# Parameter and skip-term work of a two-branch state-space convolution moved off VectorE, with a redrawn order of work

## The chip, the cores and the metric

The kernel runs on one core of one Trainium2 chip. The metric is the device time of one execution in microseconds; lower is better. PE is the matrix engine (PEld its weight loads), DVE the vector engine, ACT the scalar engine, POOL GpSimd, and SP the engine that issues the DMAs here.

## The reference

Two state-space convolutions, A (S4) and B (S4D), read the same input `x` of length L = 2048 and D = 512 channels, each with N = 128 states per channel, and a gate mixes them:

```python
dt = jnp.exp(log_dt)[:, None]
A = A_re + 1j * A_im
P = jnp.exp((dt * A)[:, :, None] * l[None, None, :])
K = jnp.einsum("dn,dnl,dn->dl", Cc, P, dt * Bc).real      # branch A
...
K = 2.0 * jnp.einsum("dn,dnl->dl", C, P).real              # branch B
...
y = irfft(rfft(K, 2 * L) * rfft(u_t, 2 * L))[..., :L] + u * Dskip
...
g = sigmoid((x * gate_w).sum(-1, keepdims=True))
return g * a + (1 - g) * b
```

The skip term `u * Dskip` is a convolution with a kernel that has `Dskip` at lag 0, so it can be added to `K` at that one lag.

## The kernel before, in words

All arithmetic is fp32. The work is cut into four quarters of 128 channels and two branches: eight units `(q, k)`. A unit has eight chunks of 16 channels.

**Parameters of a quarter** (`params_t`, L366, and `params_c`, L405). States lie on the 128 partitions, channels on the columns, 256 columns for both branches. The raw rows arrive by DMA in a buffer of the pool AB. `params_t` spreads dt over the partitions: DVE makes two diagonal tiles (L370), a matmul with ones puts the spread steps into a PSUM bank (L375), ACT copies them to SBUF as `dtb` (L378), and the bank is free again. DVE then forms the decay rates `al` (L396) and the phases `pi` (L384 to L391) from `dtb`. `params_c` forms C times B (L415 to L418, DVE), magnitude and angle of the product (L425 and L426 on ACT, L431 to L436 on DVE, L444 to L446 on ACT), the amplitudes `pf` (L452 to L456, DVE), and the starting phases `fi` (L460 to L468, DVE; L476 to L480, POOL). Intermediates lie in SBUF tiles called p.

**Anchors** (L488). DVE scales `al` (L501, L502), and ACT takes 28 columns of exponentials per channel (L514) into an AB buffer; POOL multiplies the amplitudes in (L530).

**Chunk** (L535). POOL makes the phases x (L558 to L580) and the magnitudes E (L591, L599), ACT the four tables of sines, each in a PSUM bank (L609 to L617; one in the SBUF tile scs where the table DP gives its product to POOL), DVE or POOL the products Qt, Dt, Pt, Ct (L621 to L639), PE the kernel block `K` in PSUM (L654). ACT copies it to SBUF (L665), one or two chunks at a time, and DVE adds the skip values at column 31 of every channel's 64, lag 0 (L669).

**Transform.** Stage 1 (L692) transforms `K`, or the input, into F; the eviction of each bank is on DVE (L703) or ACT (L705), as the bit tables EV and EU say. `stage2` (L755) runs the forward step (L714), the complex product with the transformed input (L775, L778, DVE), the inverse step (L786, L787) and ACT's copy back into F (L792). `final` transposes on DVE (L808), runs the last matmuls (L814), applies the gate (L828, L830, L891, L856) and writes out.

**What sets the order.** A planner (`Plan.run`, L143) lists every operation with an engine, a cost and a due time, simulates the five queues with the buffers of each pool, and always starts the operation with the earliest due time among those whose inputs and buffers are ready. The order that comes out is the program order of each engine; on the chip each engine runs its queue in that order. So costs, latencies, due times and the numbers of buffers decide the order, though none of them is an instruction. PSUM is one pool of eight banks. A change of ACT's function table costs an extra instruction (ACT_TABLE_LOAD); SWITCH is the penalty that the planner puts on it.

Of the kernel before, what the change touches and what calls it, by code (L numbers as in the profile page):

```python
# [54 lines left out]
MT = 0.3  # L55
MA = 0.0
MV = 0.0
MG = 1.0
MD = 0.0
LAT = {"T": 0.2 + MT, "A": 0.14 + MA, "V": 0.13 + MV, "G": 0.08 + MG, "D": 0.95 + MD}  # L60
# [1 line left out]
LAG = (1.2, 0.75, 0.25, 0.4, 0.35, 0.35, 0.65, 0.55)
FSP = (0.6, 0.8, 1.1, 1.0, 1.3, 1.6, 0.9, 0.1)
YSP = (0.8, 0.8, 0.8, 0.8, 0.4, 0.8, 0.5, 0.2)
UDS = (-0.4, 0.2, 4.2, 0.7)
USP = (0.3, 0.8, 1.1, 0.9)
GD = 2.8
GSP = 0.3
DP = (1, 87, 20, 255, 128, 127, 13, 149)
# [1 line left out]
TWD = 1.4
UAHEAD = 0.5
UPRE = 0.7
WPRE = 0.8
AC = 5.0
AC2 = 4.0
PT = 3.0
PC = 3.0
# [1 line left out]
CV = 0.03  # L80
CD = 0.0
CK = 0.08
CE = 0.1
CS = 0.28
FW = 0.0
# [30 lines left out]
class Plan:  # L116
# [30 lines left out]
    def run(self):  # L147
# [15 lines left out]
        while n < len(self.ops):  # L163
            nxt = 1e30
            for e in at:
# [35 lines left out]
                if e == "T":  # L201
                    k = int((now - 0.14) / 3.413)
                    if k > win:
                        cold = (cold and busy < 0.8 * 3.413) or busy < 0.45 * 3.413
                        if k > win + 1:
                            left = max(0.0, at["T"] - 3.413 * (win + 1) - 0.14)
                            cold = cold or left < 0.45 * 3.413
                        win, busy = k, max(0.0, min(at["T"], now) - 3.413 * k - 0.14)
                    if cold:
                        cost *= 2  # L210
                    dens = 0.75 if o.cost in (1.27, 1.53) else 0.95
                    busy += dens * min(cost, 3.413 * (k + 1) + 0.14 - now)
# [35 lines left out]
def gated_s4_mix(ctx: ExitStack, tc: tile.TileContext, ins: dict, out: bass.AP):  # L248
# [111 lines left out]
    def params_t(q, due):  # L360
# [22 lines left out]
        theta = (
            (0.34, lambda: V.scalar_tensor_tensor(_flat(th()), _flat(th()), 1.0 / (2 * PI), dtb.t, ALU.mult, ALU.mult)),  # L384
            (0.2, lambda: V.tensor_scalar(t(), th(), MAGIC, MAGIC, ALU.add, ALU.subtract)),
            (0.34, lambda: V.tensor_tensor(th(), th(), t(), ALU.subtract)),
            (0.2, lambda: V.tensor_scalar(piv()[:, :, :, 0], th(), TWO32 / 2, None, ALU.mult)),
            (0.2, lambda: V.tensor_scalar(t(), th(), 64.0, MAGIC, ALU.mult, ALU.add)),
            (0.2, lambda: V.tensor_scalar(t(), t(), MAGIC, None, ALU.subtract)),
            (0.34, lambda: V.scalar_tensor_tensor(_flat(t()), _flat(th()), 64.0, _flat(t()), ALU.mult, ALU.subtract)),  # L390
            (0.2, lambda: V.tensor_scalar(piv()[:, :, :, 1], t(), TWO32, None, ALU.mult)),  # L391
# [11 lines left out]
    def params_c(q, due):  # L403

        w, d = raw[q], prm[q]  # L405
        t0, t1, t2, t3, fi = Buf("p"), Buf("p"), Buf("p"), Buf("p"), Buf("fi")
# [4 lines left out]

        def prod():
            W = rawv(w)
            CC = W[:, 4:8:2, :]
# [1 line left out]
            e.tensor_tensor(p3(t1), CC, W[:, 9:11, :], ALU.mult)
# [13 lines left out]
        ratio = (  # L430
            (0.34, lambda: V.tensor_tensor(p3(t0), aa(), p3(t2), ALU.max)),  # L431
            (0.34, lambda: V.tensor_tensor(p3(t1), aa(), p3(t2), ALU.min)),
            (0.34, lambda: V.tensor_tensor(p3(t2), p3(t2), aa(), ALU.is_gt)),
            (0.2, lambda: V.tensor_scalar(aa(), p3(t0), 1e-37, None, ALU.max)),
            (1.67, lambda: V.reciprocal(aa(), aa())),
            (0.34, lambda: V.tensor_tensor(aa(), p3(t1), aa(), ALU.mult)),  # L436
        )
# [21 lines left out]
        octants = (
            (0.2, lambda: V.tensor_scalar(x0(), aa(), -1.0 / PI, 0.25, ALU.mult, ALU.add)),  # L460
            (0.34, lambda: V.tensor_tensor(x0(), x0(), x2(), ALU.mult)),
            (0.34, lambda: V.scalar_tensor_tensor(_flat(aa()), _flat(aa()), 0.5 / PI, _flat(x0()), ALU.mult, ALU.add)),
            (0.2, lambda: V.tensor_scalar(x0(), aa(), -2.0, 0.5, ALU.mult, ALU.add)),
            (0.34, lambda: V.scalar_tensor_tensor(_flat(x0()), _flat(cr()), 0.0, _flat(x0()), ALU.is_lt, ALU.mult)),
            (0.34, lambda: V.tensor_tensor(aa(), aa(), x0(), ALU.add)),
            (0.2, lambda: V.tensor_scalar(x0(), ci(), 0.0, -2.0, ALU.is_lt, ALU.mult)),
# [7 lines left out]
        def middle():  # L474
# [5 lines left out]
            G.tensor_tensor(f, f, x, ALU.add)  # L480
# [604 lines left out]
```

## Time and profile before

| | |
|---|---|
| median of three runs | 547.89 us (542.36 to 551.44) |
| the profiled execution | 545.54 us, its span 543.8 us |
| mean granted PE clock | 0.948 |
| DVE busy | 500.6 us, 92% |
| PE / PEld busy | 443.3 / 384.4 us |
| POOL busy | 417.6 us, 77% |
| ACT busy | 411.8 us, 76% |
| DMA | 74.71 MB, 137 GB/s in the mean |

A row of instructions reads: line, engine, operation, output<-inputs by tile name, shapes, count | busy us, mean ns of one | idle time of the engine just before them, and what ended it. A row of one line by itself reads: minimum/median/maximum ns, first and last start. A row of stretches reads: from:to, its length, then the busy time of each engine with its number of instructions, the granted clock, the DMA share and GB/s; asked for one engine and one tile it has only that engine's busy time in instructions that touch the tile. A row of waits reads: who <- for whom: us in total, times, longest. ps is a PSUM bank. Busy times of successive DVE instructions overlap a little (0.68 us busy for a step of 0.60).

### The profile page before, as it was taken

How to read it: one execution, taken by the hardware profiler on the slowest of the kernel's cores; microseconds unless marked ns; L12 is line 12 of the kernel's file. 1: busy time of each engine (PE TensorE's matmuls, PEld its weight loads, DVE VectorE, ACT ScalarE, POOL GpSimd, SP SyncE). 2: the span in 40 equal slices, each digit the busy share in tenths (PEclk: the TensorE clock that was granted, in tenths of full speed). 3: DMA queues.
4: the chain of work that ended last, by engine and by line, in shares of the span. 5: the costliest groups of instructions: out<-in, count | busy, mean ns of one | idle time of the engine just before them, and what ended most of it. 6: DMA issues, size and time to landing. Idle time of an engine off the chain costs nothing. (4 is left out here: it accounts for less than half of the span.)

```text
span 543.8 us, 18151 instructions
## 1 busy us (share of the span) xinstructions
PE 443.3 (82%) x7640; PEld 384.4 (71%) x7640; DVE 500.6 (92%) x789; ACT 411.8 (76%) x779; POOL 417.6 (77%) x348
## 2 busy tenths in 40 slices
PE   2687977859887876868886995949899889999994
PEld 1686877759786655657676884949689668987981
DVE  6988989998989879999999999999899988999855
ACT  5799948859999765869786996847978989775224
POOL 2499979858997995677998499585999999994002
PEclk9979978989999997989998998878999999999999
DMA  8827343634334561522342474212345253422642
GB/s 284 320 70 228 116 150 94 196 101 139 118 98 137 186 220 40 161 94 86 134 153 66 151 264 140 71 30 83 133 139 154 96 175 106 155 80 86 220 143 80
DMA packets 35747, 74.71 MB, mean 137 GB/s; under 512 B 3792, under 2 KB 4176, under 8 KB 35408
## 3 DMA queue, kind: packets, MB, share of 16 engines
q1 hardware_dynamic: 35664, 73.54, 41.0%
q8 instruction: 60, 0.98, 0.8%
q14 instruction: 23, 0.19, 0.1%
HBM read 53.60 MB, written 19.92 MB: 135 GB/s over the span
## 5 line engine op out<-in xcount | busy, mean ns | idle before, releaser
L599 POOL TENSOR_TENSOR E<-AB 128x1024 f32<-128x1024 f32 x64 | 125.9, 1967 | 0.2
L786 PE MATMUL ps<-z,c_t 128*128 128x128 f32 x512 | 104.6, 287 | 14.1 <-DVE z L775 7.4
L714 PE MATMUL ps<-F,c_g 128*128 128x128 f32 x768 | 105.0, 287 | 9.6 <-DVE Qt L624 3.4
L714 PEld LDWEIGHTS ps<-F,c_g 128*128 128x128 f32 x768 | 95.6, 198 | 19.6 <-DVE Qt L624 3.6
L787 PE MATMUL ps<-z,c_t 128*128 128x128 f32 x512 | 101.6, 281 | 1.5 <-DVE z L778 1.4
L692 PE MATMUL ps<-w,K 128*64 128x128 f32 x1024 | 73.0, 298 | 31.2 <-DVE K L669 22.1
L786 PEld LDWEIGHTS ps<-z,c_t 128*128 128x128 f32 x512 | 79.1, 195 | 25.4 <-DVE z L775 8.6
L692 PEld LDWEIGHTS ps<-w,K 128*64 128x64 f32 x1024 | 62.4, 150 | 38.3 <-DVE K L669 24.8
L580 POOL TENSOR_TENSOR x<-pi,c_tm 128x512 int32<-128x512 int32 x64 | 69.1, 1080 | 20.0 <-ACT ps L613 14.4
L787 PEld LDWEIGHTS ps<-z,c_t 128*128 128x128 f32 x512 | 79.5, 196 | 2.5 <-DVE z L778 2.5
L634 DVE TENSOR_TENSOR Pt<-ps,E 128x1024 f32<-128x1024 f32 x64 | 77.6, 1212 | 2.7 <-PE ps L654 1.9
L654 PE MATMUL ps<-Pt,Ct 128*32 128x64 f32 x2048 | 66.0, 227 | 11.0 <-DVE Ct L639 8.3
L591 POOL TENSOR_TENSOR E<-AB 128x512 f32<-128x512 f32 x64 | 69.5, 1087 | 2.8 <-ACT AB L514 2.3
L571 POOL TENSOR_TENSOR x<-gh 128x512 int32<-128x512 int32 x64 | 69.4, 1085 | 0.1
L611 ACT ACTIVATE x<-x 128x1024 f32<-128x1024 int32 x64 | 68.0, 1063 | 1.6
L630 POOL TENSOR_TENSOR Dt<-scs,E 128x512 f32<-128x512 f32 x31 | 40.2, 1297 | 35.0 <-issue 26.6
L654 PEld LDWEIGHTS ps<-Pt,Ct 128*32 128x32 f32 x2048 | 47.9, 113 | 24.8 <-DVE Ct L639 12.5
L654 PE MATMUL ps<-Qt,Dt 128*32 128x64 f32 x2048 | 64.6, 224 | 0.0
L792 ACT COPY F<-ps 128x512 f32<-128x512 f32 x64 | 37.5, 587 | 31.3 <-PE ps L787 27.1
L514 ACT ACTIVATE AB<-al 128x128 f32<-128x128 f32 (+1 forms) x160 | 55.0, 535 | 5.2 <-DVE fi L468 3.0
L609 ACT ACTIVATE ps<-x 128x512 f32<-128x512 int32 x64 | 38.7, 604 | 22.1 <-DVE z L778 9.3
L775 DVE TENSOR_TENSOR z<-ps,U 128x512 f32<-128x512 f32 x64 | 43.4, 678 | 11.2 <-DMA U<-ud 9.1
(113 smaller groups left out, 898.9 us busy)
## 6 DMA issues: line engine op xcount, KB each, us to landing
U<-ud SPq DMA_DIRECT2D x64, 512.0 KB, 3.7
ud<-z SPq DMA_DIRECT2D x32, 256.0 KB, 2.7
U<-in_u SPq DMA_DIRECT2D x16, 256.0 KB, 4.0
ud<-z SPq DMA_DIRECT2D x32, 128.0 KB, 3.1
U<-in_uT SPq DMA_DIRECT2D x8, 512.0 KB, 4.0
c_t<-in_c_t SPq DMA_DIRECT2D x1, 3072.0 KB, 10.5
w<-st SPq DMA_DIRECT2D x12, 256.0 KB, 4.1
st<-w SPq DMA_DIRECT2D x12, 256.0 KB, 3.0
```

What stands on the lines that cost most here:

```text
L514: A.activation(dst()[..., i], src(), AF.Exp, scale=sg * float(t0 + dt * i))
L571: G.tensor_tensor(xi()[:, :, 1, :].rearrange("n c (a b) -> n c a b", a=4), t[:, :, 0:4].unsqueeze(3).to_broadcast([P, NCK, 4, 8]), t[:, :, ...
L580: lambda: G.tensor_tensor(xi()[:, :, 0, :], d["piv"]()[:, k, ch, 0].unsqueeze(2).to_broadcast([P, NCK, NJ]), tm[:, 0:NJ].unsqueeze(1).to_b ...
L591: G.tensor_tensor(Ev()[:, :, 0, :].rearrange("n c (a b) -> n c a b", a=4), A1()[:, ch, ::-1].unsqueeze(3).to_broadcast([P, NCK, 4, 8]), BB ...
L599: G.tensor_tensor(Ev()[:, :, 1:3, :].rearrange("n c w t -> n c (w t)"), AA()[:, ch].rearrange("n c w a -> n (c w) a").unsqueeze(3).to_broa ...
L611: op("A", 0.95, e, lambda: A.activation(x.t, x.v(dt=I32), AF.Abs), w=[x])
L634: lambda: V.tensor_tensor(qv(Pt), tv(cf).unsqueeze(2).to_broadcast([P, NCK, 2, NJ]), Ev()[:, :, 0:2, :], ALU.mult),
L654: T.matmul(K4[32 * b : 32 * b + 32, g, :], tv(lw)[:, 4 * g + b, :], qv(rw)[:, 4 * g + b].rearrange("n h t -> n (h t)"), start=(lw is Ct), ...
L692: T.matmul(b.t[64 * d : 64 * d + 64, 128 * g : 128 * g + 128], Kv[:, g, :], w1[:, d, :], start=True, stop=True,)
L714: T.matmul(pairs(b.t[:, NCH * mm : NCH * mm + NCH]), Gw[:, 4 * mg + mm, :], Fv(F)[:, :, 4 * mg + mm, :], start=True, stop=True,)
L786: T.matmul(hb.t[:, cs], Tw[:, m, 0:128], Z1.t[:, cs], start=True, stop=False)
L787: T.matmul(hb.t[:, cs], Tw[:, m, 64:192], Z2.t[:, cs], start=False, stop=True)
```

## The change

Six things change.

1. **Skip term.** The add on DVE (L669) is gone. A matmul of the identity with the skip values, 8 or 4 columns, accumulates them in the PSUM bank of `K` behind the last product; ACT's copy follows. The products set the start flag only on the first matmul group of a bank, and the second chunk of a pair is held behind the first.
2. **Phases and decay rates.** DVE reads the spread steps from the PSUM bank instead of `dtb`, and leaves its intermediates in that bank; one phase operation fewer.
3. **Magnitudes, angles, amplitudes, starting phases.** One operand or the result of nearly every DVE operation lies in a PSUM bank instead of a p tile. Counts stay nearly the same.
4. **C times B** goes from DVE to POOL (PV is dropped).
5. **Anchors.** The product with `dtb` goes from DVE to POOL, the factor 64 from DVE to ACT.
6. **All tables and costs are drawn anew**: due times, latencies, the penalty SWITCH, the eviction bits EV, EU, ZU and FE, the pairing KP, the choice DP of Dt's engine; the planner's model of a cold PE goes.

Counted over the whole program: DVE goes from 791 to 742 instructions, with 14 more F evictions, 5 more z evictions and 36 skip adds fewer; ACT from 26 to 34 table loads, with K copies of 512 columns 28 to 18 and of 256 columns 8 to 28; POOL gets 20 more instructions; PE gets 46 matmuls more. Dt stays 33 on DVE and 31 on POOL. The DMAs are the same.

The core of the diff:

```diff
-EV = (88, 248, 8, 136, 132, 112, 8, 84)
-EU = (246, 122, 10, 210)
+EV = (107, 88, 23, 227, 242, 179, 160, 170)
+EU = (236, 180, 57, 122)
...
-KP = (4, 4, 4, 1, 4, 4, 4, 3)
+KP = (2, 4, 4, 1, 1, 1, 2, 3)
...
-SWITCH = 0.4
+SWITCH = 0.262
...
-            (0.34, lambda: V.scalar_tensor_tensor(_flat(th()), _flat(th()), 1.0 / (2 * PI), dtb.t, ALU.mult, ALU.mult)),
-            (0.2, lambda: V.tensor_scalar(t(), th(), MAGIC, MAGIC, ALU.add, ALU.subtract)),
...
+            (0.35, lambda: V.scalar_tensor_tensor(_flat(th()), _flat(th()), 1.0 / (2 * PI), b.t[:, 0:256], ALU.mult, ALU.mult)),
+            (0.35, lambda: V.tensor_scalar(h(), th(), MAGIC, MAGIC, ALU.add, ALU.subtract)),
...
-        each("V", due, theta, r=[dtb], w=[(w, ((0, 2),)), t1, pi])
+        each("V", due, theta, w=[(w, ((0, 2),)), t1, pi, b])
...
-        t0, t1, t2, t3, fi = Buf("p"), Buf("p"), Buf("p"), Buf("p"), Buf("fi")
+        t0, t1, t2, b, fi = Buf("p"), Buf("p"), Buf("p"), bank(), Buf("fi")
...
-        op("V" if PV else "G", 1.1 if PV else 2.2, due, prod, w=[rows, t0, t1])
+        op("G", 2.2, due, prod, w=[rows, t0, t1])
...
-            (0.34, lambda: V.tensor_tensor(p3(t0), aa(), p3(t2), ALU.max)),
+            (0.35, lambda: V.tensor_tensor(p3(t0), aa(), b0(), ALU.max)),
...
-        def spread():
-            if k == 1:
-                V.tensor_tensor(a1(), a1(), d["dtb"].t[:, NCH:], ALU.mult)
-            V.tensor_scalar(al.t[:, NCH : 2 * NCH], a1(), 64.0, None, ALU.mult)
-
-        op("V", 0.35 if k else 0.14, due, spread, r=[d["dtb"]] if k else [], w=[al])
+        if k == 1:
+            op("G", 0.45, due, lambda: G.tensor_tensor(a1(), a1(), d["dtb"].t[:, NCH:], ALU.mult), r=[d["dtb"]], w=[al])
+        op("A", 0.2, due, lambda: A.activation(al.t[:, NCH : 2 * NCH], a1(), AF.Copy, scale=64.0), w=[al])
...
-                            start=(lw is Ct),
-                            stop=(lw is Dt),
+                            start=(lw is Ct and g + ko == 0),
+                            stop=False,
...
+            if last:
+                T.matmul(
+                    kg.t[:, 0:n].rearrange("n (c s) -> n c s", s=NS)[:, :, 31], ident,
+                    tap[:, 2 * q + k, 4 * (c + 1) - n // NS : 4 * (c + 1)], start=False, stop=True,
+                )
...
-        op("V", 0.08, due + CE, lambda: V.tensor_tensor(tap0(), tap0(), tap[:, 2 * q + k, 4 * c1 : 4 * c + 4], ALU.add), r=[tapB], w=[K])
```

Three places of the order. In the rows, the number behind a tile's name tells buffers apart, and ps_110 to ps_117 are the eight PSUM banks.

First, the skip term early in the program. On DVE before, between products of the next chunks:

```order
L630 TENSOR_TENSOR Dt_77<-ps_112,E_73 128x512
L746 COPY z_87<-ps_114 128x512
L634 TENSOR_TENSOR Pt_79<-ps_111,E_73 128x1024
L669 TENSOR_TENSOR K_82<-K_82,dskip 128x8
L639 TENSOR_TENSOR Ct_80<-ps_110,E_73 128x512
```

On PE in the change, behind the last products of a pair (second chunk, bank ps_116) and two matmul groups ahead of stage 1:

```order
L638 MATMUL ps_116<-Pt_79,Ct_80 32x64 x4
L638 MATMUL ps_116<-Qt_76,Dt_78 32x64 x4
L647 MATMUL ps_116<-dskip,c_id 128x8
L681 MATMUL ps_110<-w_129,U_88 64x128 x8
L681 MATMUL ps_114<-w_129,U_89 64x128 x8
L681 MATMUL ps_116<-w_129,K_83 64x128 x8
```

The step has left DVE's queue; between the products and stage 1 of `K` now stands one short matmul and ACT's copy.

Second, the parameters of the second quarter. On DVE before (AB_70 holds the raw rows):

```order
L396 TENSOR_TENSOR al_106<-AB_70,dtb_99 128x128
L384 SCALAR_TENSOR_TENSOR AB_70<-AB_70,dtb_99 128x256
L415 TENSOR_TENSOR p_94<-AB_70 128x256
L416 TENSOR_TENSOR p_97<-AB_70 128x256
L417 TENSOR_TENSOR AB_70<-p_94 128x128
L418 TENSOR_TENSOR AB_70<-p_97 128x128
```

On POOL in the change, C times B stands between the last magnitudes of one chunk and the phases of the next:

```order
L581 TENSOR_TENSOR E_74<-AB_69 128x16x64
L399 TENSOR_TENSOR p_96<-AB_70 128x256
L400 TENSOR_TENSOR p_93<-AB_70 128x256
L401 TENSOR_TENSOR AB_70<-p_96 128x128
L402 TENSOR_TENSOR AB_70<-p_93 128x128
L612 TENSOR_TENSOR Dt_78<-scs_81,E_74 128x512
L562 TENSOR_TENSOR x_71<-pi_100,c_tm 128x16x32
```

Four instructions have gone from DVE's queue into POOL's, ahead of the next chunk's Dt and x.

Third, the start of PE's queue, where the steps are spread. Before:

```order
L375 MATMUL ps_110<-p_93,ones 128x256
L375 MATMUL ps_111<-p_96,ones 128x256
L375 MATMUL ps_112<-p_93,ones 128x256
L692 MATMUL ps_113<-w_129,U_88 64x128 x8
L692 MATMUL ps_115<-w_129,U_88 64x128 x8
```

In the change:

```order
L356 MATMUL ps_110<-p_95,ones 128x256
L356 MATMUL ps_111<-p_96,ones 128x256
L356 MATMUL ps_112<-p_97,ones 128x256
L356 MATMUL ps_113<-p_95,ones 128x256
L681 MATMUL ps_114<-w_129,U_88 64x128 x8
L681 MATMUL ps_115<-w_129,U_88 64x128 x8
```

All four quarters are now spread at the head. Before, ACT's copy to `dtb` was the bank's only reader. Now ps_111, ps_112 and ps_113 are read by DVE at row 109, 250 and 420 of its 666 rows, when the phases of the second, third and fourth quarter are formed, and but for ACT's copies to `dtb` no other operation has these banks until then.

More of the change, by code (lines that the diff above doesn't have):

```diff
@@ L54 @@
 CAPS = {"sc": SC, "kg": KG, "kh": KH, "fb": 8}
[L55 to L60, printed above, removed]
-SWITCH = 0.4
[L62 to L69, printed above, removed]
-GWD = -7.0
[L71 to L78, printed above, removed]
-CA = 0.24
[L80 to L85, printed above, removed]
+LAT = {'T': 0.5, 'A': 0.29, 'V': 0.13, 'G': 1.19, 'D': 0.77}
+SWITCH = 0.262
+LAG = (1.38, 0.8, 0.58, 1.0, 0.48, -0.08, 0.32, 0.72)
+FSP = (0.44, 0.89, 0.89, 0.71, 0.93, 1.75, 0.88, -0.78)
+YSP = (1.07, 1.17, 0.53, 1.11, 0.29, 0.78, 1.15, 0.71)
+UDS = (0.28, 0.51, 4.29, 0.35)
+USP = (-1.54, 0.94, 1.27, 0.24)
+GD = 2.667
+GSP = 0.39
+DP = (4, 79, 18, 219, 18, 150, 103, 215)
+GWD = -7.0
+TWD = 1.26
+UAHEAD = 0.301
+UPRE = 0.727
+WPRE = 0.404
+AC = 5.449
+AC2 = 5.494
+PT = 5.285
+PC = 2.064
+CA = 0.24
+CV = 0.074
+CD = -0.176
+CK = 0.0
+CE = 0.0
+CS = 0.0
+FW = 0.035
 def _flat(t):
@@ L200, in run @@
                     table, cost = o.func, cost + 1.3
[L201 to L212, printed above, removed]
                 at[e] = now + cost
@@ L300, in gated_s4_mix @@
     w1_in, w1_inB = load("c_w1", [P, 4, 64], -9.5)
-    tap, tapB = load("dskip", [P, 2 * NQ, 32], -0.9)
+    tap, tapB = load("dskip", [P, 2 * NQ, 32], -9.3)
     gw, gwB = load("gate_w", [P, NQ], -0.8)
@@ L457, in params_c @@
         )
+        x0, x2 = b0, lambda: p3(t2)
         octants = (
[L460 to L464, printed above, removed]
@@ L465, in params_c @@
-            (0.34, lambda: V.tensor_tensor(aa(), aa(), x0(), ALU.add)),
-            (0.2, lambda: V.tensor_scalar(x0(), ci(), 0.0, -2.0, ALU.is_lt, ALU.mult)),
-            (0.34, lambda: V.scalar_tensor_tensor(_flat(aa()), _flat(x0()), 1.0, _flat(aa()), ALU.add, ALU.mult)),
-            (0.2, lambda: V.tensor_scalar(fi.v("n (k c) -> n k c", dt=I32, k=2, c=NCH), aa(), TWO32, None, ALU.mult)),
-        )
-        each("V", due, mixed, r=[dtb, t3], w=[t0, t1, pf])
-        each("V", due, octants, w=[rows, t0, t2, fi])
+            (0.35, lambda: V.tensor_scalar(x0(), aa(), -1.0 / PI, 0.25, ALU.mult, ALU.add)),
@@ L474, in middle @@
+            (0.35, lambda: V.scalar_tensor_tensor(b1(), x0(), 1.0, aa(), ALU.add, ALU.mult)),
+            (0.35, lambda: V.tensor_scalar(fi.v("n (k c) -> n k c", dt=I32, k=2, c=NCH), b1(), TWO32, None, ALU.mult)),
+        )
+        each("V", due, mixed, r=[dtb, t0], w=[b, pf])
+        each("V", due, octants, r=[t2], w=[rows, b, fi])
         def middle():
@@ L480, in middle @@
             G.tensor_tensor(f, f, x, ALU.add)
-        op("G", 1.3, due, middle, r=[d["pi"], tmB], w=[t1, fi])
+        op("G", 3.5, due, middle, r=[d["pi"], tmB], w=[t1, fi])
         d["fi"] = fi
-    anch, step, Kt, kgs = {}, {}, {}, [None]
+    anch, step, Kt, kgs, first = {}, {}, {}, [None], [None]
     def anchors(q, k, due):
@@ L587, in chunk @@
         )
-        op("G", 1.0, due + 0.005, turns, r=[gh], w=[(x, h1)])
+        op("G", 1.03, due + 0.005, turns, r=[gh], w=[(x, h1)])
         def below():
@@ L657, in products @@
                             qv(rw)[:, 4 * g + b].rearrange("n h t -> n (h t)"),
-                            start=(lw is Ct),
-                            stop=(lw is Dt),
-                        )
-        op("T", 1.53, due + CK, products, r=[Ct, Pt, Dt, Qt], w=[(kg, kreg)])
+                            start=(lw is Ct and g + ko == 0),
+                            stop=False,
+                        )
+            if last:
[3 more added lines that the diff above has]
+                )
+        opened = [first[0]] if two and c % 2 else ()
+        first[0] = op("T", 1.06, due + CK, products, r=[Ct, Pt, Dt, Qt, tapB, identB], w=[(kg, kreg)], after=opened)
         if not last:
```

109 lines of the change are left out of this document (56 added, 53 removed).

## The prediction

> **What bounds the kernel now.** I read the page first, then the busy time by stretch, then the waits. Sums are made against the profiled run (545.54 us, its span 543.8); the median of the three runs, 547.89, lies 2.35 higher.
>
> ```profile
> PE 443.3 (82%) x7640; PEld 384.4 (71%) x7640; DVE 500.6 (92%) x789; ACT 411.8 (76%) x779; POOL 417.6 (77%) x348
> DVE  6988989998989879999999999999899988999855
> ```
>
> ```profile
> core 0: us, PE busy (x) PEld busy (x) DVE busy (x) ACT busy (x) POOL busy (x), PEclk, DMA share, GB/s
> 30.00:505.00 475.00, 398.46 (x7263) 346.83 (x7260) 450.75 (x685) 381.44 (x695) 402.27 (x327) 0.95 0.40 128
> 505.00:530.00 25.00, 25.00 (x216) 23.37 (x216) 16.66 (x29) 5.42 (x10) 0.00 (x0) 1.00 0.51 180
> 530.00:544.00 14.00, 6.41 (x46) 2.83 (x42) 7.81 (x13) 5.58 (x24) 3.85 (x3) 0.91 0.21 77
> ```
>
> There are three stages: a head to 30 us, a stretch of 475 us with all the table chunks, and a tail of 39 us. In the stretch DVE is busy 450.75 of 475 us, 95%; the others follow with POOL 85%, PE 84%, ACT 80%. The tail belongs to PE (25.00 of 25 us) and then to the last evictions. So DVE sets the pace of the stretch, but POOL and PE are only some 50 us behind it: what is taken off DVE pays until one of them is full.
>
> **What leaves DVE.**
>
> ```profile
> L669 DVE TENSOR_TENSOR K<-K,dskip x36: 111/506/3920, 48.3 to 502.1; 128x8 f32<-128x8 f32 x28, 128x4 f32<-128x4 f32 x8
> ```
>
> ```profile
> 30.00:505.00 475.00, 24.56 (x36) 0.95 0.40 128
> ```
>
> The skip term adds 8 or 4 columns in place, and takes 111 ns at best, 506 in the median and 3920 at worst; its sum in the stretch (second row, instructions on K) is 24.56 us. All of it goes. The parameter work shows the same spread:
>
> ```profile
> 30.00:505.00 475.00, 55.63 (x78) 0.95 0.40 128
> 30.00:505.00 475.00, 15.35 (x12) 0.95 0.40 128
> L416 DVE TENSOR_TENSOR p<-AB x4: 418/846/2172, 7.0 to 331.6; 128x256 f32<-128x256 f32 x4
> L386 DVE TENSOR_TENSOR AB<-AB,p x4: 412/425/426, 10.8 to 340.1; 128x256 f32<-128x256 f32 x4
> L434 DVE TENSOR_SCALAR AB<-p x4: 280/282/295, 14.8 to 342.8; 128x256 f32<-128x256 f32 x4
> L435 DVE RECIPROCAL AB<-AB 128x256 f32<-128x256 f32 x3 | 5.2, 1743 | 0.0
> L502 DVE TENSOR_SCALAR al<-al 128x128 f32<-128x128 f32 x6 | 3.9, 658 | 0.1
> L621 DVE TENSOR_TENSOR Qt<-ps,E 128x512 f32<-128x512 f32 x62 | 42.0, 678 | 1.9 <-ACT ps L609 1.7
> L891 DVE SCALAR_TENSOR_TENSOR st<-ps,gs,st 128x128 f32<-128x128 f32 x44 | 12.2, 342 | 0.0
> ```
>
> Instructions that touch p (first row, 78) and dtb (second, 12) take 55.63 + 15.35 us in the stretch, the reciprocals and the x64 add 5.2 + 3.9, and I estimate 4.5 for the nine left over (0.5 each, between the quiet 0.28 and L502's 0.66): 84.6 us for three quarters of the channels. A 256-column product takes about 420 ns when nothing is in its way, and up to 2172. Instructions that have one operand in PSUM do not spread: 62 of L621 mean 678 ns, the 128-column ones of L891 342. On the line through these two a 256-column one costs 342 + 336/3 = 454 ns. After the change a quarter has 24 such instructions (10.9 us), three of 128 columns (1.0) and the reciprocal (1.7): 13.7 us, 41 for three. DVE sheds 84.6 - 41 = 43.6. One form has no row, a single SBUF source with the result in PSUM (L369 and four more per quarter): it lies between the quiet 282 of L434 and the 846 of L416's median. I take 454, the PSUM line; over 15 instructions the ends are 2.6 us less and 5.9 more.
>
> [...]
>
> **What DVE gets.** The redrawn tables put 14 more F evictions and 5 more z evictions on it.
>
> ```profile
> L703 DVE COPY F<-ps 128x512 f32<-128x512 f32 x35 | 23.5, 680 | 1.4 <-PE ps L692 1.4
> ```
>
> 19 x 0.680 = 12.9. DVE in the stretch: 450.75 - 24.56 - 43.6 + 12.9 = 395.5. At today's 95% that takes 417 us, 58 less. This is the most that the change can bring.
>
> **What POOL gets.**
>
> ```profile
> L480 POOL TENSOR_TENSOR fi<-fi,p 128x256 int32<-128x256 int32 x3 | 2.2, 730 | 5.3 <-DVE fi L468 5.2
> L630 POOL TENSOR_TENSOR Dt<-scs,E 128x512 f32<-128x512 f32 x31 | 40.2, 1297 | 35.0 <-issue 26.6 <-ACT scs L610 7.0 <-POOL E L599 0.5
> L580 POOL TENSOR_TENSOR x<-pi,c_tm 128x512 int32<-128x512 int32 x62 | 66.9, 1079 | 16.3 <-ACT ps L613 14.4 <-PE ps L787 1.9
> ```
>
> Per quarter it takes two 256-column products (730 ns each by L480) and three of 128 columns (0.45 on the line 730 to 1297): 2.8 us, 8.4 in the stretch, so 410.7. At its order it stands between chunks, and an E or x of the next chunk waits behind it; DVE and ACT have work of earlier chunks meanwhile, without that cover it is 2.8 us a quarter again. POOL's idle time today is before L630 (35.0) and L580 (16.3): it waits for buffers that the chunk pipeline behind it returns late. That pipeline runs through DVE, so I expect most of it to go.
>
> How full can POOL get?
>
> ```profile
> 30.00:60.00 30.00, 27.13 (x604) 24.93 (x600) 25.92 (x40) 28.09 (x47) 29.77 (x26) 0.95 0.49 151
> 120.00:180.00 60.00, 51.77 (x929) 46.88 (x930) 56.19 (x84) 56.32 (x101) 54.50 (x45) 0.97 0.39 125
> 240.00:300.00 60.00, 48.42 (x915) 40.68 (x914) 59.16 (x91) 49.59 (x100) 52.95 (x43) 0.97 0.34 109
> 300.00:360.00 60.00, 50.97 (x882) 44.30 (x882) 58.47 (x85) 49.64 (x89) 47.61 (x38) 0.92 0.45 148
> 420.00:480.00 60.00, 52.77 (x990) 46.07 (x988) 56.38 (x86) 52.98 (x100) 58.07 (x49) 1.00 0.40 128
> ```
>
> 99%, 91%, 88% and 97% in its better stages, 93% over them, 79% in a stage with parameters. At 93% the 410.7 us need 441.6: 33.4 less than 475. DVE would then be at 90%.
>
> **ACT and PE.**
>
> ```profile
> L609 ACT ACT_TABLE_LOAD x9 | 11.5, 1283 | 2.1 <-DVE Pt L634 1.8 <-DVE Qt L624 0.2
> L705 ACT COPY F<-ps 128x512 f32<-128x512 f32 x57 | 32.9, 583 | 16.3 <-PE ps L692 16.2
> L665 ACT COPY K<-ps 128x512 f32<-128x512 f32 x28 | 16.4, 589 | 0.9 <-PE ps L654 0.7
> L665 ACT COPY K<-ps 128x256 f32<-128x256 f32 x8 | 3.0, 380 | 5.5 <-PE ps L654 5.5
> L521 ACT ACTIVATE al<-al 128x128 f32<-128x128 f32 x3 | 0.9, 313 | 0.0
> ```
>
> ACT: 8 more table loads (10.3), 19 evictions fewer (-11.1), K copies 28 + 8 now 18 + 28 (-5.9 + 7.6), the x64 scaling (8 x 0.313 = 2.5): +3.4, 384.8 in the stretch, 87% of 441.6. It has room.
>
> ```profile
> PE ps L692 <- DVE K L669: 22.1, 12, 5.8
> PE ps L692 <- DVE Qt L624: 7.4, 3, 6.0
> PE ps L786 <- DVE Qt L624: 4.0, 1, 4.0
> ```
>
> ```profile
> 513.18 0.22 PE ps L786 x2
> ```
>
> PE gets 46 identity matmuls. The trace has none with 4 or 8 columns; a pair with 128 x 128 weights passes in 0.22 us (the chain), so at most 10.1 us by that row and, if hidden, nothing: 398.46 to 408.6, 93% of 441.6, as full as POOL. It gains the first row: 22.1 us in which stage 1 stood for K to come back from DVE; ACT's copy is then the last step. PE is not pacing, so this is slack for it, not a term.
>
> **Head and tail.** Head: the first quarter's products go to POOL, which is idle there, and the two size steps now stand behind 20 exponentials that ACT must run in any case; I put it at nothing. Tail: by the order 32 forward matmuls and 36 inverse pairs stand behind the last stage 1 in both kernels: nothing.
>
> **The price of the banks.** The change reads the spread steps dt from PSUM until the last phase op, so its order parks three of the eight banks from the head, each until its quarter's phases are done; before, ACT's copy freed them at once.
>
> ```profile
> 76.85 0.42 DVE L384 SCALAR_TENSOR_TENSOR AB<-AB,dtb 128x256 f32<-128x256 f32 x1
> 199.17 1.28 DVE L384 SCALAR_TENSOR_TENSOR AB<-AB,dtb 128x256 f32<-128x256 f32 x1
> ```
>
> The second quarter's phases begin today at 76.85 us, the third's at 199.17, the fourth's near 330 (L416's last start is 331.6): five banks are left until about 80 us, six until 200, seven until 335. The two Qt rows above are waits for a bank: L692 and L786 read no Qt. I grant the 50 us with five banks no gain: about 3.4 of the 33.4 lost. Sum: 545.5 - 33.4 + 3.4 = **515.5**.
>
> **Rivals.** (1) All of DVE's relief arrives, since the pipeline frees POOL wholly: 545.5 - 58 = 487. For: POOL at 97 to 99% in two stages. Against: PE would need 98% too. (2) Slower: the parked banks. Waits for banks that DVE reads stand today at 7.4 + 4.0 on PE and, by the next rows, 9.3 + 4.1 + 2.7 on ACT:
>
> ```profile
> ACT ps L609 <- DVE z L778: 9.3, 3, 5.1
> ACT ps L609 <- DVE Dt L630: 4.1, 1, 4.1
> ACT ps L617 <- DVE Ct L639: 2.7, 1, 2.7
> ```
>
> 27.5 us with eight banks. If five to seven banks until 335 us make them 2.5 times as long, 41 us come on top of 515.5: 556.5, and it turns slower from 30. Against: a faster DVE frees banks sooner. (3) No change: POOL's waits do not come from DVE, and its 8.4 us are added to a stretch as long as now: 554. Against: L580 waits for ACT's L613, which waits for banks and x.
>
> **How the numbers follow.** Forecast 0.60, rival 1 0.17, rival 2 0.13, rival 3 0.10. The forecast's own range is 502 (POOL at 96%) to 535 (at 89%). The range runs from rival 1, 487, to POOL at 88%, its stage from 240 us, with the 3.4 for the banks: 541. A measurement here can tell about 2% from no change, 537 to 559 around the median: faster 0.77 (forecast and rival 1), within 0.15 (rival 3, half of rival 2), slower 0.08.
>
> **What would show it.** Right: DVE's share of the stretch below 92% and POOL's above 90%; no parameter row on DVE above 600 ns in the mean but the reciprocal; PE's wait for K at ACT, under 10 us; the stretch some 30 us shorter, the tail within 2 of 39. Wrong: POOL still near 85% (rival 3), waits of PE and ACT for Qt, Ct or Dt readers above 50 us before 335 us (rival 2), or parameter rows that still spread to 2 us (the relief itself).

## The result, and the profile after

The changed kernel takes 521.53 us in the median of four runs (520.79 to 523.44) against 547.34 (542.36 to 551.44): a ratio of 0.9563, 95% interval 0.9492 to 0.9634. The profiled run of the changed kernel took 520.79 us, its span is 519.0. The forecast was 515.5. Ratios here and below leave out executions in a slower state, such as the one of 551.44 us of the kernel before.

First the page of the changed kernel, the busy time of each engine and DVE's slices:

```profile
PE 453.8 (87%) x7732; PEld 393.0 (76%) x7732; DVE 444.5 (86%) x740; ACT 418.1 (81%) x786; POOL 423.1 (82%) x368
DVE  6658898887959879999999999999998978999854
```

DVE's total fell from 500.6 to 444.5 us. To see where the span went I cut both traces at the same points of the program: the start of POOL's first product (onto x) of the fifth chunk and of the last one. Busy time by stretch, the kernel before:

```profile
0.00:49.50 49.50, 30.65 (x416) 27.16 (x418) 40.76 (x87) 37.59 (x82) 30.76 (x35) 0.93 0.67 234
49.50:489.60 440.10, 366.61 (x6668) 319.67 (x6664) 420.02 (x630) 355.54 (x652) 376.70 (x307) 0.95 0.39 127
489.60:543.80 54.20, 46.08 (x563) 37.56 (x561) 39.78 (x74) 18.67 (x48) 10.15 (x9) 0.98 0.39 133
```

The changed kernel, cut at the same chunks (columns as before: PE, PEld, DVE, ACT, POOL, clock, DMA):

```profile
0.00:57.10 57.10, 41.28 (x570) 36.08 (x570) 40.00 (x85) 41.79 (x90) 32.99 (x40) 0.91 0.67 233
57.10:466.00 408.90, 368.43 (x6678) 321.31 (x6678) 367.78 (x591) 356.81 (x645) 379.79 (x321) 0.95 0.42 133
466.00:519.00 53.00, 44.15 (x485) 35.64 (x484) 36.70 (x66) 19.55 (x52) 10.29 (x9) 0.98 0.40 130
```

The same chunks take 408.9 us instead of 440.1, 31.2 less; the head is 7.6 longer, the end 1.2 shorter. 7.6 - 31.2 - 1.2 = -24.8, the whole difference of the spans. In the long part DVE went from 95% (420.02 of 440.1) to 90%, POOL from 86% to 93%, PE from 83% to 90%, ACT from 81% to 87%.

### The profile page after: what moved, and what is told of

Its sections match the earlier page's. It is cut to its first block, busy times and chain, and to the rows that moved or that the text cites. A ratio compares the mean times of both kernels' runs of the same rounds, so it can differ in the third digit from the quotient of the medians.

```text
span 519.0 us, 18350 instructions
## 1 busy us (share of the span) xinstructions
PE 453.8 (87%) x7732; PEld 393.0 (76%) x7732; DVE 444.5 (86%) x740; ACT 418.1 (81%) x786; POOL 423.1 (82%) x368
## 4 chain that ended last, share of the span: by engine, by line
PE 40%; DVE 21%; ACT 20%; issue 6%; DMA 5%; POOL 5%; SPq 0%; POOLq 0%; DVEq 0%; ACTq 0%
PE ps L681 9%; PE ps L703 8%; PE ps L775 7%; PE ps L776 6%; PE ps L638 6%; PE ps L803 3%; ACT AB L496 2%; DMA AB<-in_prm 2%; ACT ps L591 2%; ACT x L593 2%; DVE F L797 2%; DVE Ct L621 2%; DVE Pt L616 2%; DVE z L767 2%; DVE F L692 2%
## 5 line engine op out<-in xcount | busy, mean ns | idle before, releaser
L562 POOL TENSOR_TENSOR x<-pi,c_tm 128x512 int32<-128x512 int32 x64 | 67.8, 1060 | 20.8 <-ACT ps L595 18.7
L681 PE MATMUL ps<-w,K 128*64 128x128 f32 x1024 | 68.9, 284 | 10.2 <-ACT K L657 6.3
L681 PEld LDWEIGHTS ps<-w,K 128*64 128x64 f32 x1024 | 57.6, 141 | 19.5 <-ACT K L657 8.2
L573 POOL TENSOR_TENSOR E<-AB 128x512 f32<-128x512 f32 x64 | 68.4, 1070 | 4.2 <-ACT AB L496 2.4
L553 POOL TENSOR_TENSOR x<-gh 128x512 int32<-128x512 int32 x64 | 68.3, 1068 | 1.9 <-ACT ps L599 1.8
L638 PEld LDWEIGHTS ps<-Qt,Dt 128*32 128x32 f32 x2048 | 49.2, 114 | 0.0
L603 DVE TENSOR_TENSOR Qt<-ps,E 128x512 f32<-128x512 f32 x64 | 43.4, 679 | 5.3 <-POOL E L581 3.8
```

The source lines that it names most:

```text
L553: G.tensor_tensor(xi()[:, :, 1, :].rearrange("n c (a b) -> n c a b", a=4), t[:, :, 0:4].unsqueeze(3).to_broadcast([P, NCK, 4, 8]), t[:, :, ...
L562: lambda: G.tensor_tensor(xi()[:, :, 0, :], d["piv"]()[:, k, ch, 0].unsqueeze(2).to_broadcast([P, NCK, NJ]), tm[:, 0:NJ].unsqueeze(1).to_b ...
L573: G.tensor_tensor(Ev()[:, :, 0, :].rearrange("n c (a b) -> n c a b", a=4), A1()[:, ch, ::-1].unsqueeze(3).to_broadcast([P, NCK, 4, 8]), BB ...
L638: T.matmul(K4[32 * b : 32 * b + 32, g, :], tv(lw)[:, 4 * g + b, :], qv(rw)[:, 4 * g + b].rearrange("n h t -> n (h t)"), start=(lw is Ct an ...
L681: T.matmul(b.t[64 * d : 64 * d + 64, 128 * g : 128 * g + 128], Kv[:, g, :], w1[:, d, :], start=True, stop=True,)
```

## The experiments

All but runs 6, 11 and 12 keep the changed kernel's order on every engine and change only what its instructions do. The kernel before is timed beside each group; ratios are against it.

**1. The skip term back on DVE, in place.**

```diff
-            if last:
-                T.matmul(
-                    kg.t[:, 0:n].rearrange("n (c s) -> n c s", s=NS)[:, :, 31], ident,
-                    tap[:, 2 * q + k, 4 * (c + 1) - n // NS : 4 * (c + 1)], start=False, stop=True,
-                )
...
+            A.copy(K.t[:, 0:n], kg.t[:, 0:n])
+            tap0 = K.t[:, 0:n].rearrange("n (c s) -> n c s", s=NS)[:, :, 31]
+            V.tensor_tensor(tap0, tap0, tap[:, 2 * q + k, 4 * (c + 1) - n // NS : 4 * (c + 1)], ALU.add)
```

> The changed kernel with its own order kept on every engine; only the skip term goes back: no identity matmul, and DVE adds the 8 or 4 columns into K right after ACT's copy (46 adds). Relief theory (what came off DVE made the gain): some 25 us come back on DVE (0.5 us each, as in the kernel before), DVE is then at some 420 us of the stretch, 94%, and PE stands for K again: 530 to 537. Order theory (the new due times and eviction engines made the gain, the ops only cleared the way): 519 to 525.

Measured: ratio 0.9999 (0.9955 to 1.0044), span 540.5. The whole gain of the change is gone with this one part. All adds of this run, and then what DVE and POOL did around one of them:

```profile
L655 DVE TENSOR_TENSOR K<-K,dskip x46: 143/668/1948, 52.3 to 496.6; 128x4 f32<-128x4 f32 x28, 128x8 f32<-128x8 f32 x18
```

```profile
305.30 1.95 DVE L655 TENSOR_TENSOR K<-K,dskip 128x4 f32<-128x4 f32 x1
307.17 0.68 DVE L606 SCALAR_TENSOR_TENSOR Qt<-ps,E 128x512 f32<-128x512 f32 x1
```

```profile
305.27 1.96 POOL L581 TENSOR_TENSOR E<-AB 128x1024 f32<-128x1024 f32 x1
307.18 1.06 POOL L562 TENSOR_TENSOR x<-pi,c_tm 128x512 int32<-128x512 int32 x1
```

An add of four columns takes 1.95 us: it begins 0.03 us after a POOL instruction of 1.96 us and ends when that one ends. This is no accident of one row: in the trace 42 of the 46 adds end within 0.06 us behind the end of a POOL instruction that ran beside them; the four others took 143 to 173 ns. Two explanations were left for the 20 us: that DVE loses this time, or that K now goes through DVE's queue and PE waits for it (PE waits 21.7 us for this line). Runs 2 and 3 part them.

**2. The same add on DVE, but in PSUM.** There is no identity matmul here either, and the add stands before ACT's copy, so K goes through DVE as in run 1, but one operand is not in SBUF.

```diff
+            tap0 = kg.t[:, 0:n].rearrange("n (c s) -> n c s", s=NS)[:, :, 31]
+            V.tensor_tensor(tap0, tap0, tap[:, 2 * q + k, 4 * (c + 1) - n // NS : 4 * (c + 1)], ALU.add)
+            A.copy(K.t[:, 0:n], kg.t[:, 0:n])
```

> The changed kernel with its own order kept; no identity matmul: DVE adds the skip term into the products' PSUM bank, between PE's last product and ACT's copy of K (46 adds of 8 or 4 columns, one operand in PSUM). In the run with the add in SBUF every add ended within 0.03 us of the end of the POOL instruction that ran beside it. Port theory (an all-SBUF instruction of DVE stands until POOL's instruction is over, one with PSUM does not): the adds fall from 0.67 us in the median to about 0.1, some 5 us on DVE in all, and the time is 519 to 527. Chain theory (K going through DVE's in-order queue is what costs, in whatever memory): 533 to 545, as with the add in SBUF.

Measured: 525.17 us, ratio 0.9625 (0.9573 to 0.9677), inside the 519 to 527 of what the expectation calls the port theory.

```profile
L654 DVE TENSOR_TENSOR ps<-ps,dskip 128x4 f32<-128x4 f32 x28 | 4.5, 160 | 0.0
L654 DVE TENSOR_TENSOR ps<-ps,dskip 128x8 f32<-128x8 f32 x18 | 2.9, 164 | 1.8 <-PE ps L638 1.8
```

160 ns each, and DVE waits 1.8 us for PE in all. A POOL instruction ran beside 44 of these 46 adds, and none of them took more than 175 ns. ("Every add" and "0.03 us" in the expectation are too neat: run 1 has 42 of 46, within 0.06 us. And "port" is a name: these runs show when DVE stands and for how long, not why.) Whether the add in PSUM is worse than the identity matmul at all these runs don't settle, since the two intervals overlap.

**3. The add in SBUF, its result thrown away.** The identity matmul stays, PE waits for nobody new.

```diff
             A.copy(K.t[:, 0:n], kg.t[:, 0:n])
+            tap0 = K.t[:, 0:n].rearrange("n (c s) -> n c s", s=NS)[:, :, 31]
+            V.tensor_tensor(spare[:, 0 : n // NS], tap0, tap[:, 2 * q + k, 4 * (c + 1) - n // NS : 4 * (c + 1)], ALU.add)
```

> The changed kernel as it is, identity matmuls and all, and in addition DVE does the 46 adds after ACT's copy of K but writes them to a spare tile that nobody reads: DVE's work and its waits are there, PE's wait for DVE is not. If DVE's lost time makes the 20 us of the run with the add in SBUF: 535 to 545. If PE's wait for K (26.5 us there, 21 times) makes them: 521 to 527. Half of each: about 531.

Measured: ratio 0.9894 (0.9814 to 0.9974), span 542.6. It is DVE's lost time that costs, not PE's wait for K: no instruction waits for these adds. DVE is 29.4 us busier (473.9 against 444.5) and also stands 12.0 us before the adds for ACT's copy of K, so the loss is not all beside POOL:

```profile
L662 DVE TENSOR_TENSOR spare<-K,dskip x46: 144/639/1997, 51.8 to 499.6; 128x4 f32<-128x4 f32 x28, 128x8 f32<-128x8 f32 x18
```

**4. The parameter work back in SBUF.** b0, b1 and h move to a free part of the raw parameter buffer w, and the two instructions that read dt read its SBUF copy.

```diff
-        b0 = lambda: b.t[:, 0:256].rearrange("n (k c) -> n k c", k=2)
-        b1 = lambda: b.t[:, 256:512].rearrange("n (k c) -> n k c", k=2)
+        b0 = lambda: w.t[:, 2048:2304].rearrange("n (k c) -> n k c", k=2)
+        b1 = lambda: w.t[:, 2304:2560].rearrange("n (k c) -> n k c", k=2)
...
-            (0.35, lambda: V.scalar_tensor_tensor(_flat(th()), _flat(th()), 1.0 / (2 * PI), b.t[:, 0:256], ALU.mult, ALU.mult)),
+            (0.35, lambda: V.scalar_tensor_tensor(_flat(th()), _flat(th()), 1.0 / (2 * PI), dtb.t, ALU.mult, ALU.mult)),
```

> The changed kernel with its own order kept; only the operands of the parameter work go back to SBUF (dt from its SBUF copy, the scratch halves in a free part of the raw parameter buffer), C x B stays on POOL. Relief theory: DVE's parameter rows spread again to 0.6 to 1.3 us in the mean, some 25 to 36 us more on DVE: 532 to 545. Order theory: 519 to 525. Bank theory (the parked banks cost time in the changed kernel): the banks of the spread steps and of the scratch come free at once, and the time falls to 512 to 518 although DVE gets dearer.

Measured: ratio 1.0008 (0.9963 to 1.0054), span 542.2: this part alone is worth the whole gain too. The bank theory, which wanted a shorter time, is not borne out in this order. Two lines in the changed kernel, then the same two in this run:

```profile
L415 DVE TENSOR_TENSOR p<-AB,ps x4: 410/413/422, 16.4 to 343.7; 128x256 f32<-128x256 f32 x4
L418 DVE TENSOR_SCALAR ps<-p x4: 428/428/428, 17.7 to 344.9; 128x256 f32<-128x256 f32 x4
```

```profile
L415 DVE TENSOR_TENSOR p<-AB x4: 881/1190/2028, 16.8 to 363.5; 128x256 f32<-128x256 f32 x4
L418 DVE TENSOR_SCALAR AB<-p x4: 294/1146/1256, 19.2 to 368.0; 128x256 f32<-128x256 f32 x4
```

With a PSUM operand the four quarters differ by 0 to 12 ns. In SBUF the same work takes 294 to 2028 ns. The wait beside POOL is the same as for the adds: the five longest parameter instructions of this run (2.03 to 2.13 us) each began 0.06 to 0.36 us behind the start of a POOL product onto E and ended 0.15 to 0.28 us behind its end. That two parts are each worth the whole gain says that these prices hold in this order only, and that they need not add up.

**5. Both, and the C x B products back on DVE.** The edits of runs 1 and 4, and G.tensor_tensor is V.tensor_tensor in prod().

> The changed kernel with its own order kept on every engine, and the skip add, the SBUF operands and the C x B products all back on DVE: what is left of the change is its due times, its eviction engines and the two al steps. Relief theory: DVE carries some 60 us more than its 395 in the stretch, more than the stretch holds: 548 to 562, no better than the kernel before. Order theory: 521 to 530.

Measured: ratio 1.0494 (1.041 to 1.0578), span 570.1, 51.1 over the changed kernel and above either range. Run 1 alone adds 21.5 to the span, run 4 alone 23.2; the products would be the other 6.4 if the three simply add, but 2.6 by the medians, so this remainder can't be told from noise. So the changed kernel's order with nearly the operations of before (not its eviction engines and al steps) is some 26 us worse than before's own order: due times and operations belong together. What before's operations would give if the planner drew its order for them from the new due times was not tried.

**6. The new operations with the due times of before.** All tables of constants and the latencies go back; the planner draws the order anew.

```diff
-EV = (107, 88, 23, 227, 242, 179, 160, 170)
-EU = (236, 180, 57, 122)
+EV = (88, 248, 8, 136, 132, 112, 8, 84)
+EU = (246, 122, 10, 210)
...
```

> The changed kernel's operations and costs with the due times, the eviction engines and the latencies of the kernel before (its F and z evictions go back from DVE to ACT, 19 of them); the planner draws the order from these. Relief theory: the ops bring most of it even so, 518 to 532. Order theory: 538 to 550, hardly below the kernel before.

Measured: 536.77 us, ratio 0.9844 (0.9783 to 0.9906): between both ranges. The operations bring about 10 us under the old due times (8.5 by the ratio, 5 to 12 by its interval), and about 15 more come with the new ones. The split is rough, since each order is a single draw of the planner: run 12, with the same due times and nearly the same instructions, comes out 31 us away.

**7. to 10. A little off one engine at a time.** These ask which engine paces the changed kernel. Part of the result is left out, as each expectation says.

The core of each edit, in the order m_pool, m_dve, m_pe, m_act (m is 13 there, and the other three sines are alike):

```diff
-                Ev()[:, :, 1:3, :].rearrange("n c w t -> n c (w t)"),
+                Ev()[:, 0 : NCK - 2, 1:3, :].rearrange("n c w t -> n c (w t)"),
...
-                qv(Pt), tv(cf).unsqueeze(2).to_broadcast([P, NCK, 2, NJ]), Ev()[:, :, 0:2, :], ALU.mult
+                qv(Pt)[:, 0:12], tv(cf)[:, 0:12].unsqueeze(2).to_broadcast([P, 12, 2, NJ]), Ev()[:, 0:12, 0:2, :], ALU.mult
...
-                for lw, rw in ((Ct, Pt), (Dt, Qt)):
+                for lw, rw in ((Ct, Pt), (Dt, Qt))[: 2 if g < 2 else 1]:
...
-        op("A", 0.56, e, lambda: A.activation(tv(sf), xi()[:, :, 0, :], AF.Sin, scale=SCL), r=[(x, h0)], w=[sf], func="S")
+        op("A", 0.56, e, lambda: A.activation(tv(sf)[:, 0:m], xi()[:, 0:m, 0, :], AF.Sin, scale=SCL), r=[(x, h0)], w=[sf], func="S")
```

> The changed kernel with its own order; each of the 64 larger POOL products on E covers 14 of 16 columns groups, the rest of E stays at a filled-in zero (that part of the result is left out). It takes 0.245 us off each, 15.7 us off POOL in all, and nothing off another engine. If POOL paces the stretch (91% busy): 12 to 16 us shorter, 506 to 510. If PE and DVE (90% and 89%) hold it as much: 2 to 7 us shorter, 515 to 520.

> The changed kernel with its own order; each of the 64 products on Pt (DVE) covers 12 of 16 groups of columns, the rest of Pt stays at a filled-in zero (that part of the result is left out): some 0.28 us off each, 18 us off DVE, nothing off another engine. If DVE still paces the changed kernel (its 30 us more cost 21 in the run with the spare tile, 0.7 us for each): 506 to 511. If it has come down to the level of the others, as POOL's 13.6 us less gave 2: 517 to 520.

> The changed kernel with its own order; of the 32 small products of a chunk, the eight of Dt with Qt in the upper half of K are left out (that part of the result too): about a quarter of 1.06 us, some 17 us off PE over 64 chunks. If PE paces (90% busy in the stretch): 506 to 511. If it is one of several level engines: 517 to 520.

> The changed kernel with its own order; the four sines of a chunk cover 13 of 16 groups of columns from the third chunk on, the rest holds what the bank held before (that part of the result is left out): some 0.08 us off each, 20 us off ACT. ACT is the least busy of the four (86% of the stretch): 516 to 521 by the busy shares. If the chain of a chunk through ACT (POOL's angles, ACT's sines, DVE's products, PE) sets the pace and not a full engine: 508 to 514.

Measured, with the engine's busy time from the first line of each page (the changed kernel: PE 453.8, DVE 444.5, ACT 418.1, POOL 423.1):

| run | taken off | span | median | ratio, 95% interval |
|---|---|---|---|---|
| changed kernel | | 519.0 | 521.53 | 0.9563, 0.9492 to 0.9634 |
| m_pool | POOL 13.1 | 519.0 | 519.52 | 0.9512, 0.9456 to 0.9568 |
| m_dve | DVE 14.7 | 513.4 | 516.25 | 0.9465, 0.9408 to 0.9522 |
| m_pe | PE 18.0 | 514.9 | 515.84 | 0.9449, 0.9384 to 0.9514 |
| m_act | ACT 16.4 | 511.9 | 514.93 | 0.9445, 0.9383 to 0.9506 |

```profile
PE 449.0 (87%) x7732; PEld 389.6 (75%) x7732; DVE 444.9 (86%) x740; ACT 418.5 (81%) x786; POOL 410.0 (79%) x370
```

```profile
PE 446.9 (87%) x7732; PEld 388.2 (76%) x7732; DVE 429.8 (84%) x740; ACT 417.4 (81%) x786; POOL 423.4 (82%) x369
```

```profile
PE 435.8 (85%) x6708; PEld 374.5 (73%) x6708; DVE 444.4 (86%) x740; ACT 417.1 (81%) x786; POOL 423.1 (82%) x368
```

```profile
PE 447.3 (87%) x7732; PEld 389.9 (76%) x7732; DVE 443.9 (87%) x740; ACT 401.7 (78%) x786; POOL 422.9 (83%) x368
```

The four lines are m_pool, m_dve, m_pe and m_act. Each interval touches that of the changed kernel, so none of these gains is proved by itself; what is excluded is what "this engine paces" asked for, a gain of nearly all that was taken off. m_pool fell into its range for level engines, the other three between their two ranges. PE's total also falls by 4.8 to 6.9 us in the three runs that leave its matmuls alone, at granted clocks of 0.958 to 0.967 against 0.952. By the medians DVE, PE and ACT give 0.3 to 0.4 us for each us, POOL 0.15 (2.0 of 13.1) and by the span nothing. ACT, the least busy of the four, gave no less than the others, so the busy shares don't rank them. By these runs no single engine paces the changed kernel; every chunk goes through all four in turn.

**11. The head.** One swap in ACT's order; `early[0]` is the operation with the last exponentials of the second unit's anchors.

```diff
...
     order = pl.run()
+    i = order.index(early[0])
+    j = max(n for n in range(i) if order[n].eng == "A")
+    order.insert(j, order.pop(i))
```

> The changed kernel with one swap in ACT's order in the head: the eight last exponentials of the second unit's anchors run before the F eviction for whose matmul ACT stands 3.3 us at 33 us; nothing else is moved. ACT's first sines of the third chunk come some 3.3 us earlier. If the 7 us by which the changed kernel is late at its fifth chunk are carried to the end: 517 to 519. If the stretch takes them up anyway: 520.5 to 522.5.

Measured: 519.4 us, ratio 0.951 (0.9455 to 0.9565), between the two ranges, which neither confirms nor excludes the 3 us. The trace says why it could not: the sines did not come earlier. ACT in the changed kernel, and then in this run:

```profile
33.13 0.59 ACT L694 COPY F<-ps 128x512 f32<-128x512 f32 x1 [3.31 <-PE ps L681]
33.61 3.74 ACT L496 ACTIVATE AB<-al 128x256 f32<-128x256 f32 x8
37.14 1.61 ACT L737 COPY z<-ps 128x512 f32<-128x512 f32 x3
38.77 1.28 ACT L592 ACT_TABLE_LOAD   x1
```

```profile
34.06 0.59 ACT L694 COPY F<-ps 128x512 f32<-128x512 f32 x1 [0.30 <-PE ps L681]
36.06 0.59 ACT L737 COPY z<-ps 128x512 f32<-128x512 f32 x1 [1.41 <-PE ps L703]
37.85 0.59 ACT L737 COPY z<-ps 128x512 f32<-128x512 f32 x1 [1.20 <-PE ps L703]
38.74 0.59 ACT L737 COPY z<-ps 128x512 f32<-128x512 f32 x1 [0.31 <-PE ps L703]
39.35 1.28 ACT L592 ACT_TABLE_LOAD   x1
```

The exponentials moved out of the way, and the three z evictions behind them waited for PE instead.

**12. Without the parked banks.** theta and al read dt from its SBUF copy, h gets a bank of its own, and the planner draws a new order.

```diff
-        h = lambda: b.t[:, 256:512].rearrange("n (k c) -> n k c", k=2)
+        hb = bank()
+        h = lambda: hb.t[:, 0:256].rearrange("n (k c) -> n k c", k=2)
...
```

> The changed kernel's operations with the spread steps read from their SBUF copy and the phase scratch in a bank of its own that is taken only when the phases begin: the three banks parked from the head are free until then, two DVE instructions per quarter are all-SBUF again (about 1 us each in the mean). The planner draws the order anew with the same due times. Bank theory (the parked banks cost 3.4 us or more): 510 to 518. If waits for banks were no longer than before (24 us of such waits on PE and ACT against 27.5): 521 to 527, the redrawing and the two instructions being all that shows.

Measured: 552.98 us, ratio 1.0149 (1.0085 to 1.0212), outside both ranges. The engines do about the same work (DVE 450.3, PE 460.5, POOL 424.0 us busy by its page), but stand for one another far longer; three of its waits:

```profile
PEld ps L640 <- DVE Ct L623: 28.7, 14, 6.7
POOL x L564 <- ACT ps L597: 26.5, 6, 7.5
POOL x L555 <- ACT ps L601: 16.8, 6, 4.5
```

In the changed kernel PEld's wait for Ct is 5.4 us, and POOL's two waits are 18.7 and 1.8. The redrawing, the freed banks and two instructions per quarter back in SBUF came together, so the 31 us over the changed kernel are the price of all three. That the redrawing is most of it is argued from these waits; what the banks cost stays open.

## Why the prediction was right, and where it was not

**DVE's sum held, within some 3 us.** It asked for 395.5 us on DVE in the stretch from 30 us. The changed kernel has 395.21 from 30 to 475 us; ACT 384.40 where 384.8 stood, PE 402.05 (408.6), POOL 405.13 (410.7):

```profile
30.00:475.00 445.00, 402.05 (x7300) 350.69 (x7300) 395.21 (x633) 384.40 (x690) 405.13 (x342) 0.96 0.43 135
475.00:519.00 44.00, 35.82 (x330) 29.11 (x318) 27.86 (x51) 13.62 (x42) 3.93 (x3) 0.98 0.44 144
```

The cut at 475 us is the length that the forecast gave, so part of this agreement is made by the cut. From 30 us to the end of the program DVE goes from 475.22 to 423.07 us: 52.2 less, where the sum has 55.3. ACT goes up by 5.6 (3.4 foreseen), PE by 8.0 (at most 10.1) and POOL by 2.9 only (8.4 foreseen): the means of POOL's eight largest groups all fell a little, 413.4 us in the sum against 418.4. Whether DVE had held POOL up as well was not tried.

A parameter instruction of 256 columns with an operand in PSUM took 408 to 433 ns, the reciprocal apart, so the 454 of the line were a little dear. Why the relief is as large as that, the prediction did not say: it took sums and means, and left open what is "in its way" when a product takes 2172 ns instead of 420. Runs 1, 2 and 4 show what it was. With all operands in SBUF, 42 of the 46 adds of run 1 end within 0.06 us behind the end of a POOL instruction that ran beside them, and so do 28 of the 36 skip adds of the kernel before; with one operand in PSUM none took more than 175 ns, though POOL ran beside 44 of 46 (run 2). Run 4 has the wait in its longest parameter rows, 2.03 to 2.13 us, and its DVE total lies 27 us above the changed kernel's (471.9 against 444.5).

Not all work of DVE in SBUF stands like this. In the kernel before POOL ran beside 42 of the 64 transposes, and none took more than 740 ns:

```profile
L808 DVE STREAM_TRANSPOSE F<-F x64: 658/680/740, 161.6 to 534.0; 128x512 f32<-128x512 f32 x64
```

**The gain of the stretch held, the step "how full can POOL get" only as a number.** 31.2 us between the same two chunks, where the sum had 33.4 less 3.4 for the banks. The number leans on the first mark: from the seventeenth chunk to the last the gain is some 24 us, since between the fifth and the seventeenth the changed kernel only makes up for its later start. POOL did end at 93% there (379.79 of 408.9). But as a reason the step fails: with 13.1 us taken off POOL nothing of size followed (run 7). DVE led the kernel before with 95%; now four engines stand at 87% to 93%, and each gives less than half of what is taken off it. The same is seen on DVE from both sides: 29.4 us put back in run 3 (473.9 busy) cost 23.6 of span, 0.8 for each (21.1 by the medians, 0.7), and 14.7 taken off in run 8 (m_dve) gave 5.6, 0.4. That is the likely reason why rival 1 (487) did not come: between the marks 52.2 us left DVE, and 31.2 arrived.

**The term that looks mis-sized: "Head: ... I put it at nothing".** By the mark at the fifth chunk it is 7.6 us, more than the 6.0 between forecast and result. I had watched that the size step stands behind 20 exponentials, and that costs little (the last phase op of the first quarter starts at 27.73 us, before at 27.55). What I did not follow is ACT's order behind it. The three z evictions of the input's transform now stand ahead of the third chunk's first sines, and PE, which feeds them, ran at a granted clock of 0.61, where the kernel before had 0.80 (busy time of the kernel before, then of the changed one):

```profile
20.00:30.00 10.00, 3.76 (x56) 3.28 (x54) 9.62 (x18) 5.86 (x18) 5.88 (x5) 0.80 0.40 151
20.00:30.00 10.00, 5.75 (x50) 4.95 (x52) 9.53 (x21) 6.94 (x20) 5.96 (x5) 0.61 0.33 123
```

The table load for the third chunk's sines before, and POOL's wait in the changed kernel:

```profile
33.53 1.28 ACT L610 ACT_TABLE_LOAD   x1
43.57 1.06 POOL L562 TENSOR_TENSOR x<-pi,c_tm 128x512 int32<-128x512 int32 x1 [7.79 <-ACT ps L595]
```

The load comes at 38.77 us in the changed kernel, and POOL stands 7.79 us for the buffer that these sines read. That this order is the cause is argued from the rows; run 11 moved the wrong piece. By the chunk marks the two kernels are level at the seventeenth chunk (140.4 and 140.7 us), so how much of the 7.6 us would reach the end is open. Cut there, the head costs 0.3 us, and the 5.2 us that are missing (24.8 of span where the sum has 30.0) lie in the stretch: which of the two terms was mis-sized depends on the cut.

**PE and the identity matmuls.** The sum had at most 10.1 us. By their own row it is 18.3, and 46 of them are 92 instructions:

```profile
L647 PE MATMUL ps<-dskip,c_id 128*128 128x4 f32 (+1 forms) x92 | 18.3, 270 | 0.0
```

But the row overlaps its neighbours. PE's total is 10.5 us above the kernel before (453.8 against 443.3), 11.6 above run 2 without identity matmuls (442.2), and 7.3 higher in run 3 than in run 1 (454.2 and 446.9). So the bound was about right.

```profile
PE ps L681 <- ACT K L657: 6.3, 6, 2.8
```

PE's wait for K went from 22.1 us on DVE to 6.3 on ACT, as foreseen under 10, but run 3 shows that it was not what paid. The tail was to stay as it is; from the mark at the last chunk it is 53.0 us against 54.2.

**Rival 2, the parked banks.** Waits for banks that DVE reads, in the changed kernel:

```profile
PE ps L703 <- DVE fi L453: 9.0, 3, 4.5
PE ps L703 <- DVE Pt L616: 5.5, 5, 2.3
ACT ps L592 <- DVE Ct L621: 4.6, 6, 1.7
```

With two smaller ones (2.6 and 2.2, PE for Pt) 23.9 us, against 27.5 before: not 2.5 times as long, and its 41 us did not come. Both sums pick some rows; all such rows of PE and ACT over the whole program come to some 41 us, against 51 before. The longest, behind L453, is a wait for the scratch bank of the starting phases and not for a parked one. What the parking itself costs, my 3.4 us, run 12 leaves open.

**Rival 3** falls by POOL's wait before Dt, 35.0 us before and 7.8 now:

```profile
L612 POOL TENSOR_TENSOR Dt<-scs,E 128x512 f32<-128x512 f32 x31 | 39.8, 1283 | 7.8 <-ACT scs L592 2.7 <-POOL E L581 2.2 <-POOL x L562 1.1
```

The profile puts none of the 35.0 down to DVE (26.6 are "issue"), but the wait comes back with DVE's work: 20.4 us in run 3 with the adds, 35.2 in run 5 with everything. The other wait that the prediction expected to go, before x, stayed: 16.3 us then, 18.7 now (L562 behind ACT's L595).

## What to carry to other kernels

When the same instruction of one engine takes many times its best time, look at what the other engine was doing and when the two end; here the sum to be won was the spread, and one operand in PSUM was enough to win it (adds of 160 to 164 ns in the mean in run 2, where run 1 has 668 in the median). Each us put back on DVE cost 0.7 to 0.9 us of kernel (runs 1, 3 and 4), and a us taken off any of four level engines gave less than half; take the total of the other engines as the bound, but try which of them paces before calling one of them the pacer. And where a planner's tables were drawn for one set of operations, compare a change of operations with its own tables: here the new operations under the old tables were 15 us, and nearly the old ones in the new order 51 us, worse than the matched pair, each of them a single order.
